# Fourteen matmuls of zeros ahead of TensorE's queue, and a new order table

## The chip, the cores and the metric

The kernel runs on one core of one Trainium2 chip. The metric is the device time of one execution in microseconds, the median of three runs. TensorE is called PE below, VectorE DVE, ScalarE ACT, GpSimd POOL, and SyncE, which issues all of this kernel's transfers, SP.

## The reference

Two branches over the same 2048 x 576 input are added to that input. Each row is normalized first.

```python
x = A_x                                   # (1, 2048, 576)
xn = _layernorm(x, axis=-1)
# branch A: 2-D real FFT, product with a complex filter, inverse FFT
X = rfft2(xn, axes=(-2, -1))
y = irfft2(X * (w_r + 1j * w_i), (2048, 576))
# branch B: 32 heads, each picks one of 8 x 8 = 64 experts by two argmaxes
q = einsum("nd,dhc->nhc", xn, w_q)        # c = 2 * 128
i1, t1 = top1(q[..., :128] @ k1.T)        # 8 scores
i2, t2 = top1(q[..., 128:] @ k2.T)        # 8 scores
act = gelu(einsum("nd,nhkd->nhk", xn, u[8 * i1 + i2]))
out = einsum("nhk,nhk,nhkd->nd", softmax(t1 + t2), act, v[8 * i1 + i2])   # one candidate: the softmax is 1
return x + y + out
```

## The kernel before

The 2048 rows are sixteen tiles of 128 rows (row n*16+m is row n of tile m). Both FFTs are done as dense matmuls with constant matrices, split into high and low float16 halves where precision asks for it. The stages, by the names of the functions in the code:

- `ln(t, n)`: mean and variance of n tiles, partly on DVE (`bn_stats`, `bn_aggr`), partly on ACT. From them come the scales in `rr`.
- `folds(t)`: sums and differences of a tile with its mirror image, on POOL and DVE, into a tile `A2` (the profile prints `A`, of which there are four); ACT writes the scaled matrix `Rs` and a small tile `yl`.
- `dft128(t)`: on PE two short matmuls (`Rs,yl`) and four 128 x 128 ones (`Rs,A`), float32. ACT copies the sums into `AB` and `ABL` as float16, and DVE subtracts to get the low halves. Every later transform, `d_fwd`, needs all sixteen of these.
- `fold_part(b, s)`: 32 loads `w` of `w_q`, 576 KB each, into five buffers, and four column-tiled matmuls (`w,KP`) on each. They combine `w_q` with `k1`, `k2` into one score matrix `MU`.
- `d_fwd(g)`, `s_fwd(g)`, `s_mul(g)`, `s_inv(g)`: transform along the 576 columns, along the rows, product with the filter `Wt` (on DVE, `t<-banks,wx,Wt`), and back along the rows.
- `x_t(t)`, `scores(r)`, `route(r)`, `combine(r)`: normalized tiles transposed by DMA, scores of two tiles at a time (matmuls `MU,xT`, 128 x 512), then on DVE the maxima and the coefficients, which two transposes on PE (`id,MT`) bring into `CAT`.
- `d_inv(t)`, `fin(t)`: back along the columns (`c,ABL`, `c,AB`), and at last per half tile one float32 matmul (`A,c`) and two with `vS`, an addition on DVE into `w`, and the store to `out`.

No instruction is issued as it is written. The calls `V`, `A`, `G`, `P`, `Q` only record operations in a plan. Neighbouring PE calls of one stage on one PSUM tile are joined into one operation. The table `RANK` holds one number per operation; `_Plan.forward` goes through the operations, each engine taking the ready one of lowest rank by the plan's own clock, and `_Plan.issue` then emits them in that order. So `RANK` sets the order on every engine's queue and the DMA issue order on SP, and also which PSUM bank each PSUM tile gets. Every engine executes its own queue strictly in that order. All instructions carry line L526 of the recorder in the profile, so groups are told apart by tile names.

The lines around the edit:

```python
    mxr = K([128, 10], F32, "mxr")
    G.memset(mxr, 0.0)
    used_ = []
```

`mxr` holds ten columns, one for each call of `allmax`, which takes maxima over partitions there; the tenth, `mxr[:, 9:10]`, is zero until the last of these calls.

Of the kernel before, what the change touches and what calls it, by code (L numbers as in the profile page):

```python
# [12 lines left out]
BF = mybir.dt.bfloat16  # L13
# [19 lines left out]
def _consts():  # L33
# [102 lines left out]
CHANGE = 97.0  # L136

RANK = (
# [63 lines left out]
)  # L202
LIMIT = {"x": 2, "a": 4, "b": 4, "c": 4, "s": 2, "f": 1, "m": 2}
WORDS = {"mxr": 1, "mxd": 4, "st": 48, "mv": 8, "Rs": 128, "t1": 578, "t2": 578, "A2": 578, "y": 578,
# [333 lines left out]
def _body(ctx, tc, nc, plan, a, out):  # L538
# [3 lines left out]
    V, A, G, P, Q = plan.engines  # L542
# [98 lines left out]

    mxr = K([128, 10], F32, "mxr")
    G.memset(mxr, 0.0)
    used_ = []

    def staged(f):
        def g(*args):
# [570 lines left out]
```

## Time and profile before

| | |
|---|---|
| median of 3 runs | 223.99 us (223.98 to 224.19) |
| the profiled execution | 224.18 us |
| its span, first to last instruction | 222.4 us |
| busy: PE, DVE | 197.0 us, 190.0 us |
| busy: ACT, POOL | 133.9 us, 139.8 us |
| bytes moved | 48.15 MB |
| first real matmul | 9.71 us after the span's start |
| mean granted PE clock | 0.991 |

The span is what the views below cover; 1.78 us of the execution lie outside it. A row of the timeline reads: start, length, engine, line, operation, written tile <- read tiles, size, count, and in brackets the idle time before it with what ended it. A row of the windows reads: stretch, its length, busy time of each engine with its number of instructions, the granted PE clock, the share of the DMA engines in use, GB/s. Float32 matmuls show as two instructions each.

### The profile page before, as it was taken

How to read it: one execution, taken by the hardware profiler on the slowest of the kernel's cores; microseconds unless marked ns; L12 is line 12 of the kernel's file. 1: busy time of each engine (PE TensorE's matmuls, PEld its weight loads, DVE VectorE, ACT ScalarE, POOL GpSimd, SP SyncE). 2: the span in 40 equal slices, each digit the busy share in tenths (PEclk: the TensorE clock that was granted, in tenths of full speed). 3: DMA queues.
4: the chain of work that ended last, by engine and by line, in shares of the span. 5: the costliest groups of instructions: out<-in, count | busy, mean ns of one | idle time of the engine just before them, and what ended most of it. 6: DMA issues, size and time to landing. Idle time of an engine off the chain costs nothing.

```text
span 222.4 us, 5915 instructions
## 1 busy us (share of the span) xinstructions
PE 197.0 (89%) x2274; PEld 133.6 (60%) x2274; DVE 190.0 (85%) x411; ACT 133.9 (60%) x281; POOL 139.8 (63%) x198
## 2 busy tenths in 40 slices
PE   0289598999998998889999699999999999999993
PEld 0246446785766666675745564654576565678872
DVE  1999999997579978675899989999999998997553
ACT  2279869799938887996686795646541231233320
POOL 2978986860358543794445868769566274657890
PEclk9999979999999999999999999999999999999999
DMA  7999999999999999766170621403452350278935
GB/s 169 378 426 422 406 409 403 392 338 331 302 313 406 288 316 302 193 138 180 42 197 16 160 58 35 111 0 72 92 130 87 106 162 0 60 217 263 409 119 212
DMA packets 33388, 48.15 MB, mean 217 GB/s; under 512 B 20688, under 2 KB 23504, under 8 KB 32976
## 3 DMA queue, kind: packets, MB, share of 16 engines
q1 hardware_dynamic: 33360, 47.77, 66.4%
q8 instruction: 18, 0.29, 0.5%
q14 instruction: 10, 0.08, 0.1%
HBM read 38.33 MB, written 4.72 MB: 194 GB/s over the span
## 4 chain that ended last, share of the span: by engine, by line
PE 56%; DVE 22%; DMA 8%; ACT 5%; issue 4%; POOL 2%; SPq 1%; POOLq 0%; DVEq 0%
PE banks L526 56%; DMA w<-in_wq_dram 7%; DVE t L526 6%; DVE w L526 5%; DVE MT L526 4%; DVE A L526 2%; DMA XN<-in_x_dram 2%; DVE mx L526 1%; DVE AB L526 1%; POOL yh L526 1%; ACT AB L526 1%; DVE sc L526 1%; DVE ABL L526 1%; ACT t L526 1%; ACT yl L526 1%
## 5 line engine op out<-in xcount | busy, mean ns | idle before, releaser
L526 PE MATMUL banks<-MU,xT 128*128 128x512 f16 x192 | 46.8, 379 | 0.7 <-DVE t L526 0.4
L526 POOL TENSOR_TENSOR hl<-XN,hl 128x576 f16<-128x576 f32 x16 | 21.2, 1325 | 24.8 <-ACT hl L526 24.4
L526 PE MATMUL banks<-c,AB 128*128 128x145 f16 (+1 forms) x384 | 35.3, 227 | 0.0
L526 PEld LDWEIGHTS <-xT 128*128 128x128 f16 x224 | 19.7, 98 | 24.1 <-issue 5.5
L526 PEld LDWEIGHTS <-AB 128*128 128x128 f16 x384 | 32.4, 122 | 2.8 <-issue 1.3
L526 POOL TENSOR_TENSOR t<-XN 128x289 f32<-128x289 f32 x32 | 25.3, 809 | 9.3 <-DMA XN<-in_x_dram 3.8
L526 POOL TENSOR_TENSOR A<-t 128x145 f32<-128x145 f32 (+2 forms) x48 | 28.6, 612 | 2.2 <-DVE t L526 0.7
L526 POOL TENSOR_TENSOR y<-t,t 128x289 f32<-128x289 f32 x32 | 22.3, 714 | 10.9 <-DVE t L526 10.5
L526 ACT ACTIVATE yh<-banks,sc 128x580 f32<-128x580 f32 x16 | 11.8, 744 | 24.3 <-PE banks L526 19.3
L526 DVE SCALAR_TENSOR_TENSOR t<-banks,wx,Wt 128x578 f32<-128x578 f32 x32 | 24.5, 808 | 2.0 <-PE banks L526 1.3
L526 POOL TENSOR_TENSOR yh<-y,yh 128x578 f16<-128x578 f32 x16 | 20.7, 1302 | 7.5 <-ACT yh L526 4.2
L526 DVE TENSOR_TENSOR AB<-banks,AB 128x512 f16<-128x512 f32 x32 | 21.7, 680 | 3.9 <-ACT ABL L526 3.3
L526 PE MATMUL banks<-w,KP 128*32 128x288 f32 x256 | 22.4, 449 | 2.5 <-DMA w<-in_wq_dram 1.5
L526 ACT ACTIVATE AB<-banks 128x512 f16<-128x512 f32 x32 | 19.0, 595 | 8.7 <-PE banks L526 8.7
L526 PE MATMUL banks<-Rs,yl 128*99 128x128 f32 x64 | 12.0, 317 | 12.5 <-ACT Rs L526 10.6
L526 PE MATMUL banks<-A,c 128*128 128x288 f32 x64 | 21.7, 421 | 0.5 <-ACT MT L526 0.5
L526 PE MATMUL banks<-c,ABL 99*128 99x289 f16 (+1 forms) x64 | 18.6, 291 | 1.3 <-DVE t L526 0.6
L526 PEld LDWEIGHTS banks<-Rs,yl 128*99 128x99 f32 x64 | 8.7, 186 | 16.8 <-ACT Rs L526 12.6
L526 PEld LDWEIGHTS banks<-Rs,A 128*128 128x128 f32 x128 | 16.4, 203 | 3.2 <-DVE A L526 1.4
L526 DVE TENSOR_REDUCE MT<-w 128x128 bf16<-128x896 bf16 (+1 forms) x16 | 18.2, 1142 | 0.1
L526 PE MATMUL banks<-Rs,A 128*128 128x128 f32 x128 | 18.0, 290 | 0.0
L526 POOL TENSOR_TENSOR t<-yh 128x288 f32<-128x288 f32 x16 | 11.2, 702 | 10.7 <-ACT yh L526 10.6
(106 smaller groups left out, 418.6 us busy)
## 6 DMA issues: line engine op xcount, KB each, us to landing
w<-in_wq_dram SPq DMA_DIRECT2D x32, 576.0 KB, 7.3
Wt<-in_W_dram SPq DMA_DIRECT2D x8, 578.0 KB, 4.3
w<-in_x_dram SPq DMA_DIRECT2D x8, 576.0 KB, 4.6
out_dram<-w SPq DMA_DIRECT2D x14, 288.0 KB, 3.8
XN<-in_x_dram SPq DMA_DIRECT2D x3, 1282.0 KB, 13.4
s<-in_s_dram SPq DMA_DIRECT2D x16, 192.0 KB, 3.1
XN<-in_x_dram SPq DMA_DIRECT2D x2, 641.0 KB, 5.3
c<-in_c_dram SPq DMA_DIRECT2D x1, 868.5 KB, 8.3
```

Source lines behind the costliest of these rows:

```text
L526: fn(*[x.place() if isinstance(x, _Ps) else x for x in args], **{k: x.place() if isinstance(x, _Ps) else x for k, x in kw.items()})
```

## The change

Two things. Behind the memset of `mxr` fourteen bfloat16 matmuls are recorded on PE, with a 128 x 128 stationary and a 128 x 512 moving operand, both the broadcast zero column of `mxr`. They write one PSUM bank that nothing reads. And `RANK` is a new table, which has four more entries, since the fourteen calls become four operations. The memset of `mxr` also goes ahead of that of `KP` on POOL.

```diff
     mxr = K([128, 10], F32, "mxr")
     G.memset(mxr, 0.0)
     used_ = []
+
+    zr = mxr[:, 9:10].bitcast(BF)[:, 0:1]
+    pz = PS("m", (128, 512))
+    for k in range(14):
+        P.matmul(pz, zr.to_broadcast([128, 128]), zr.to_broadcast([128, 512]), start=True, stop=True)
...
 RANK = (
-    2, 11, 10, 12, 49, 94, 8, 9, 5, 6, 3, 4, 1, 34, 38, 35, 39, 7, 0, 15, 17, 20, 13, 18, 21, 24, 23, 26, 28,
...
+    2, 15, 12, 16, 53, 98, 10, 11, 6, 8, 7, 4, 3, 39, 42, 38, 43, 1, 5, 9, 13, 14, 0, 21, 19, 24, 17, 22, 25,
```

The order on all engines is alike in the large: the same stages follow each other. It differs by small swaps nearly everywhere, and by more from the first `d_inv` on. Four places are shown. The first is the head of PE's queue in the changed kernel: the last two of the fourteen, then the first real groups (`Rs,yl` and `Rs,A2` are `dft128`, `w,KP` is `fold_part`).

```order
L526 LDWEIGHTS mxr_83
L526 MATMUL banks_66<-mxr_83 128x512
L526 LDWEIGHTS mxr_83
L526 MATMUL banks_66<-mxr_83 128x512
L526 MATMUL banks_66<-Rs_1_102,yl_1_104 99x128 x2
L526 MATMUL banks_66<-Rs_1_102,A2_1_98 128x128 x4
L526 MATMUL banks_66<-Rs_0_101,yl_0_103 99x128 x2
```

Before, the queue begins with the first `Rs,yl` row; behind it the first eight groups are the same in both.

The second place is PE's queue around `dft128(2)`, `(4)` and `(5)`, before:

```order
L526 MATMUL banks_66<-Rs_0_101,A2_2_99 128x128 x4
L526 MATMUL banks_66<-Rs_1_102,A2_1_98 128x128 x4
L526 MATMUL banks_66<-w_0_117,KP_73 32x288 x4
L526 MATMUL banks_66<-Rs_0_101,yl_0_103 99x128 x2
L526 MATMUL banks_66<-w_4_121,KP_73 32x288 x4
L526 MATMUL banks_66<-w_1_118,KP_73 32x288 x4
L526 MATMUL banks_66<-Rs_0_101,A2_0_97 128x128 x4
```

and now:

```order
L526 MATMUL banks_66<-Rs_0_101,A2_2_99 128x128 x4
L526 MATMUL banks_66<-w_4_121,KP_73 32x288 x4
L526 MATMUL banks_66<-Rs_0_101,yl_0_103 99x128 x2
L526 MATMUL banks_66<-w_0_117,KP_73 32x288 x4
L526 MATMUL banks_66<-Rs_0_101,A2_0_97 128x128 x4
L526 MATMUL banks_66<-w_1_118,KP_73 32x288 x4
L526 MATMUL banks_66<-Rs_1_102,A2_1_98 128x128 x4
```

The four matmuls of `dft128(5)` (`A2_1`) stood right behind those of `dft128(2)`; they now stand behind three groups that wait for loads of `w`, and behind `dft128(4)` (`A2_0`).

The third place is DVE's queue where `s_mul(10)` and `s_mul(11)` read PSUM (`t1`, `t2`), before:

```order
L526 SCALAR_TENSOR_TENSOR t1_1_96<-banks_66,wx_82,Wt_0_110 128x578
L526 SCALAR_TENSOR_TENSOR t2_0_105<-banks_66,wx_82,Wt_0_110 128x578
L526 SCALAR_TENSOR_TENSOR t1_0_95<-banks_66,wx_82,Wt_0_110 128x578
L526 TENSOR_TENSOR ABL_75<-banks_66,ABL_75 33x2x128
L526 TENSOR_TENSOR AB_74<-banks_66,AB_74 128x4x128
L526 TENSOR_REDUCE mx_1_128<-banks_66 128x128
L526 SCALAR_TENSOR_TENSOR t2_1_106<-banks_66,wx_82,Wt_0_110 128x578
```

and now:

```order
L526 SCALAR_TENSOR_TENSOR t2_0_105<-banks_66,wx_82,Wt_0_110 128x578
L526 SCALAR_TENSOR_TENSOR t1_1_96<-banks_66,wx_82,Wt_0_110 128x578
L526 SCALAR_TENSOR_TENSOR t1_0_95<-banks_66,wx_82,Wt_0_110 128x578
L526 SCALAR_TENSOR_TENSOR t2_1_106<-banks_66,wx_82,Wt_0_110 128x578
L526 TENSOR_TENSOR ABL_75<-banks_66,ABL_75 33x2x128
L526 TENSOR_TENSOR AB_74<-banks_66,AB_74 128x4x128
L526 TENSOR_REDUCE mx_1_128<-banks_66 128x128
```

The last of the four reads moved ahead of the evictions of `s_inv(8)` and of the maximum of `scores(1)`.

The fourth place is the end of PE's queue, from the last scores on. Behind the last `MU,xT` and `MUL,xT` matmuls stand, before, nine `d_inv`, fourteen `fin` and five pairs of transposes of `combine`; now nine `d_inv`, thirteen `fin` and three such pairs. `d_inv` goes in the order 1, 0, 3, 2, 5, 7, 4 ... before, and 0, 1, 2, 3, 4, 6, 5 ... now.

124 rows, old and new, of the table RANK are left out of this document.

## The prediction

> **What bounds the kernel now.** I read the page first (busy times, clock by slices), then the stretches of 10 us, then the chain that ended last, and at last PE's clock on a finer grid.
>
> ```profile
> span 222.4 us, 5915 instructions
> PE 197.0 (89%) x2274; PEld 133.6 (60%) x2274; DVE 190.0 (85%) x411; ACT 133.9 (60%) x281; POOL 139.8 (63%) x198
> ...
> PEclk9999979999999999999999999999999999999999
> ```
>
> No engine is busy throughout; PE and DVE come near it, so the stretches must say which of them sets the pace where.
>
> ```profile
> 0.00:10.00 10.00, 0.28 (x1) 0.29 (x2) 5.19 (x21) 2.64 (x5) 5.47 (x17) 1.00 0.84 259
> 10.00:20.00 10.00, 8.96 (x59) 6.36 (x59) 9.59 (x30) 7.49 (x23) 8.19 (x16) 1.00 1.01 419
> 20.00:30.00 10.00, 7.44 (x68) 4.49 (x60) 9.80 (x29) 8.68 (x25) 8.98 (x16) 0.87 1.02 414
> 30.00:40.00 10.00, 8.90 (x84) 6.22 (x80) 9.57 (x24) 7.84 (x22) 7.36 (x13) 0.96 1.02 404
> 40.00:50.00 10.00, 9.64 (x91) 8.02 (x84) 9.14 (x22) 8.45 (x24) 7.17 (x10) 1.00 0.99 363
> ...
> 70.00:80.00 10.00, 8.97 (x173) 6.14 (x166) 9.07 (x20) 8.08 (x18) 5.76 (x7) 1.00 1.07 318
> 80.00:90.00 10.00, 8.52 (x150) 5.94 (x148) 8.69 (x18) 7.87 (x15) 3.90 (x5) 1.00 1.07 309
> 90.00:100.00 10.00, 8.94 (x171) 7.16 (x171) 6.96 (x19) 10.00 (x21) 8.92 (x10) 1.00 0.63 154
> ...
> 120.00:130.00 10.00, 8.13 (x104) 5.14 (x99) 9.59 (x15) 7.10 (x14) 7.73 (x9) 1.00 0.40 100
> ```
>
> The columns are PE, PEld, DVE, ACT, POOL, clock, DMA share, GB/s. From 10 to 50 us DVE is busy 9.14 to 9.80 us of each 10, and the DMA engines are full (0.99 to 1.02), while PE has 0.36 to 2.56 us to spare. So in the front, where the dummies act, PE waits for others. Later PE has gaps of 1.0 to 1.9 us per 10 us in the four worst stretches.
>
> ```profile
> 46.64 20.17 PE banks L526 x262
> ...
> 134.80 31.02 PE banks L526 x361
> ...
> 197.74 21.29 PE banks L526 x174
> 219.03 0.02 issue
> 219.05 0.52 DVE w L526
> ```
>
> On the chain, PE has the long unbroken pieces, the last one up to 219.0 us. Behind the front the end is set by PE's queue and its gaps.
>
> **The fourteen matmuls.** Their cost: they need only the memset of `mxr`.
>
> ```profile
> 0.73 0.31 POOL L526 MEMSET KP<- 128x256 f32 x1 [0.29 <-POOLq L1209]
> 0.97 0.11 POOL L526 MEMSET mxr<- 128x10 f32 x1
> ...
> 183.31 2.75 PE L526 MATMUL banks<-MU,xT 128*128 128x512 f16 x12
> ...
> 9.71 1.17 PE L526 MATMUL banks<-Rs,yl 128*99 128x128 f32 x4 [9.71 <-ACT Rs L526]
> ```
>
> The memset ended at 1.08 us, behind that of `KP`; now it stands first on POOL, so the dummies start at about 0.9 us. A 128 x 512 matmul at full clock takes 2.75 / 12 = 0.23 us at most (float16 here, the nearest row), at half clock 0.46, so fourteen take 3.2 to 6.4 us and are over between 4.1 and 7.3 us. The first real matmul waits until 9.71 us for ACT's `Rs`. That idle time hides them whole: cost 0. Without it they would cost up to 6.4 us.
>
> What they could bring is the clock. The early groups are slow, the same groups later fast:
>
> ```profile
> 10.68 1.92 PE L526 MATMUL banks<-Rs,A 128*128 128x128 f32 x8
> ...
> 14.64 2.15 PE L526 MATMUL banks<-w,KP 128*32 128x288 f32 x16
> ...
> 37.84 0.68 PE L526 MATMUL banks<-Rs,yl 128*99 128x128 f32 x4
> 38.36 1.06 PE L526 MATMUL banks<-Rs,A 128*128 128x128 f32 x8
> ...
> 39.78 1.18 PE L526 MATMUL banks<-w,KP 128*32 128x288 f32 x16
> ```
>
> 1.17 against 0.68, 1.92 against 1.06, 2.15 against 1.18: half clock, though the page's clock row shows full there, since nothing changed before. The first slow groups lose 0.49 + 0.86 + 0.97 = 2.32 us on PE. Is it recovered? I laid a grid of 3.41 us over the trace, through the points at which the granted clock changes:
>
> ```profile
> 10.25:13.67 3.42, 2.47 (x12) 1.00 1.01 420
> 13.67:17.08 3.41, 3.41 (x21) 1.00 1.01 427
> ...
> 23.91:27.32 3.41, 0.99 (x11) 1.00 1.02 411
> 27.32:30.73 3.41, 3.37 (x21) 0.50 1.03 411
> ...
> 88.75:92.17 3.42, 2.64 (x49) 1.00 1.07 246
> ...
> 218.45:221.86 3.41, 0.56 (x4) 1.00 0.69 247
> 221.86:222.40 0.54, 0.00 (x0) 0.52 0.00 0
> ```
>
> After 0.99 and 0.56 us busy in a window the next one has half clock; after 2.64 the clock stays. After a full window at half clock (27.32) it is full again; 2.47 us did not lift it, for the `w,KP` row at 14.64 is still slow. So windows decide, not single gaps. The dummies fill the window up to 6.84 us (one step of the grid below 10.25) and lift the clock there. The next, 6.84 to 10.25, then holds at most 0.5 us of them plus 9.71 to 10.25: about 1.0 us, as much as the window that was followed by half clock. By these rows the clock drops again at 10.25 us and the real groups run as slow as before. I cost the effect at 0.
>
> The Trainium skill, "TensorE: Matmul & The Clock Gate", Part 1, has the same window, 3413 ns, calls it free-running, and says that the phase moves the transition from run to run; this trace has one phase only. Its list "Why this matters for your kernels" asks that PE have no gap over some 3 us between bursts; by that rule the gap of 2.4 us or more behind the dummies could still keep the clock. The trace has no gap like it at that place, so that stands as a rival below.
>
> If the clock did stay, DVE bounds what comes of it: it idles 0.41 us from 10 to 20 and 0.20 from 20 to 30, so at most 0.6 of the 2.3 us could reach the end. Bounds of this term: -0.6 to 0.
>
> **The order, front.** Around `dft128(4)` and `(5)` PE waited twice:
>
> ```profile
> 22.26 1.95 PE L526 MATMUL banks<-Rs,A 128*128 128x128 f32 x16
> 25.69 0.69 PE L526 MATMUL banks<-w,KP 128*32 128x288 f32 x8 [1.48 <-DMA w<-in_wq_dram]
> 27.36 1.17 PE L526 MATMUL banks<-Rs,yl 128*99 128x128 f32 x4 [0.98 <-ACT yl L526]
> ```
>
> The second wait is for `yl` of tile 4, which ACT now writes earlier in its queue, so the 0.98 us can go. In return `dft128(5)`, half of the x16 row that ended at 24.21, now stands behind three loads of `w`. DVE paces this stage, with 0.20 us idle, so a PE wait removed brings nothing by itself: 0, with -0.2 and the loss of the rival below as ends.
>
> **The order, middle.** The read of PSUM by `s_mul(11)` that moved ahead frees a bank for `d_fwd`, which waited for it:
>
> ```profile
> 125.06 0.80 DVE L526 SCALAR_TENSOR_TENSOR t<-banks,wx,Wt 128x578 f32<-128x578 f32 x1
> ...
> 125.92 0.28 PE L526 MATMUL banks<-c,ABL 99*128 99x289 f16 x1 [0.34 <-DVE t L526]
> ```
>
> It ran at 125.06 behind three operations; now it follows the third read directly. The 0.34 us wait on PE goes; the evictions that it passed come 0.8 us later, and no wait of PE in this stretch is put down to them. I take -0.3 (0 to -0.34).
>
> **The order, end.** Behind the last scores PE has one `fin` and two pairs of transposes less; ahead of them as much more. Total PE work is equal, so only gaps can be won:
>
> ```profile
> 193.16 0.75 PE L526 MATMUL banks<-A,c 128*128 128x288 f32 x2 [0.47 <-ACT MT L526]
> ...
> 197.74 0.28 PE L526 MATMUL banks<-c,ABL 99*128 99x290 f16 x1 [0.26 <-DVE w L526]
> ```
>
> These two, 0.73 us, were waits for a `combine` and for an eviction, and both are now spread out. I take half, -0.4 (0 to -0.73).
>
> **The many other swaps** I cannot follow one by one. They can close or open gaps of PE. The four stretches above hold 1.03 + 1.48 + 1.06 + 1.87 = 5.44 us of them; an order that closed 40% would gain 2.2, and I see no reason why one that opens as many should be excluded. I take 0 for them.
>
> **Sum.** 0 + 0 - 0.3 - 0.4 = -0.7. The profiled execution took 224.18 us (span 222.40, 1.78 outside it), so 223.5; the median of the runs, 223.99, lies 0.19 below that execution, hence 223.3 us. Measurement tells about 0.2% (0.45 us) from no change.
>
> **Rivals.** *The clock stays up.* The window behind the dummies may hold more than I count, if they run with their weight loads not overlapped, or the phase of the grid may be another. For it: the trace shows nothing between 0.99 and 2.64 us busy at full clock. Against it: DVE and DMA are full in the front. Time: 223.3 - 0.6 = 222.7.
>
> *No difference.* The dummies do nothing, and the swaps cancel. For it: the front is paced by DVE, and PE's work behind it is the same. Time: 224.0.
>
> *Slower, through `dft128(5)`.* Its sums free the buffer into which `folds(9)` is written (four `A` buffers in turn, 5 and 9 share one), and then come `dft128(9)`, `(13)`. PE reached it at about 23.2 us; now it needs three `w` groups to have landed, and one load of 576 KB at 414 GB/s takes 1.4 us by itself, so from the 25.69 above at least until 25.69 + 2 x 1.4 = 28.5, then the groups themselves: about 30 us. `folds(9)` moved back on DVE as well, so it decides only if the loads come later than about 33 us, which half clock in that very window (27.32 to 30.73) makes likelier. Then DVE, which has nothing to spare, stands still for the rest. Price: what half clock costs the groups there, 1.17 - 0.68 + 2.15 - 1.18 = 1.5 us (the row at 27.36, and sixteen `w,KP` as at 14.64), and all of it reaches the end. Time: 224.0 + 1.5 = 225.5.
>
> **Chances.** The forecast, small gains from the order without help of the clock: 0.38, of which 0.05 lies within 0.2%. Clock stays: 0.12. No difference: 0.18. Slower: 0.32. So faster 0.33 + 0.12 = 0.45, same 0.18 + 0.05 = 0.23, slower 0.32. The range: up to the third rival, 225.5; down to -2.2 for the swaps with the -0.3 of the middle taken as part of them, about 223.99 - 2.2 - 0.4 = 221.4. My forecast alone has 222.6 to 223.9.
>
> **What would show it.** Fourteen `mxr` matmuls between 0.9 and 7.3 us; then the first `Rs,A` x8 at 1.9 us (clock fell back) or near 1.06 (it stayed). The first real matmul still at about 9.7. DVE over 95% busy from 10 to 40 us; if it drops below, with a wait at `folds(9)` or `ABL`, the third rival holds. No wait of PE for `yl` near 27 us, none for `t` near 126. Wrong I would be if the swaps that I set at 0 move PE's gaps behind 50 us by more than 2 us either way.

## The result, and the profile after

The changed kernel takes 226.37 us (median), the kernel before 224.04 beside it: ratio 1.010, 95% interval 1.008 to 1.012. It is slower by some 2.3 us, outside the range that I gave. Single disturbed executions (one of 232.16 us here, later three of six of the new order alone and five of twelve with one exchange) count in the medians but are left out of this and all later ratios. The profiled execution took 226.41 us. Its page:

```profile
span 224.5 us, 5962 instructions
...
PE 200.4 (89%) x2288; PEld 134.4 (60%) x2288; DVE 192.7 (86%) x411; ACT 133.4 (59%) x281; POOL 144.7 (64%) x198
...
PEclk9959999999999999999999999999999999999999
```

PE has 3.4 us more, with 4.9 us of zeros in it. DVE has 2.7 us and POOL 4.9 us more, with the same 411 and 198 instructions as before. So the same instructions last longer. The busy time by stretches tells where. Columns: stretch, its length, busy PE, PEld, DVE, ACT, POOL (instructions), clock, DMA share, GB/s. First the kernel before, then the changed one:

```profile
0.00:62.00 62.00, 47.22 (x455) 33.71 (x459) 51.26 (x138) 45.92 (x114) 39.73 (x72) 0.97 0.98 362
...
130.00:224.00 94.00, 87.60 (x843) 58.09 (x836) 81.54 (x162) 34.95 (x69) 58.11 (x81) 0.99 0.42 125
```

```profile
0.00:62.00 62.00, 51.80 (x485) 34.88 (x486) 50.60 (x140) 45.92 (x114) 41.91 (x72) 0.94 0.99 374
...
130.00:224.00 94.00, 86.43 (x810) 57.28 (x809) 85.04 (x158) 32.54 (x66) 59.19 (x79) 1.00 0.45 125
```

Up to 62 us DVE does slightly more in less time; behind 130 us it needs 3.5 us more for fewer instructions. The times of the same pieces of work agree. The changed kernel is ahead at first: the first reads of `s_mul` behind 60 us start at 61.24 instead of 62.45, those of `s_mul(11)` at 119.18 instead of 120.95, those of `s_mul(12)` at 132.96 instead of 134.66, a lead of 1.7 us. Then it loses 3.9 us: its last `fin` starts at 221.24, where the kernel before had it at 219.05.

Which instructions grew? The forms on DVE behind 130 us, kernel before, then changed kernel (count, busy us, mean ns, idle before):

```profile
L526 DVE TENSOR_REDUCE mx<-banks 128x128 f32<-128x896 f32 x6 | 6.5, 1081 | 0.7 <-PE banks L526 0.5 <-ACT act L526 0.2
...
L526 DVE TENSOR_TENSOR w<-w,MT 128x512 bf16<-128x512 bf16 x14 | 5.4, 412 | 0.0
L526 DVE TENSOR_TENSOR w<-w,wt 128x896 bf16<-128x896 bf16 x7 | 4.3, 613 | 0.0
...
L526 DVE TENSOR_SCALAR MT<-MT 128x16 int32<-128x16 f32 x16 | 2.5, 197 | 0.0
...
L526 DVE SCALAR_TENSOR_TENSOR MT<-MT 128x64 bf16<-128x64 bf16 x7 | 1.5, 213 | 0.0
```

```profile
L526 DVE TENSOR_TENSOR w<-w,MT 128x512 bf16<-128x512 bf16 x14 | 6.8, 523 | 0.0
...
L526 DVE TENSOR_REDUCE mx<-banks 128x128 f32<-128x896 f32 x6 | 6.5, 1075 | 0.0
...
L526 DVE TENSOR_TENSOR w<-w,wt 128x896 bf16<-128x896 bf16 x6 | 4.8, 802 | 0.0
L526 DVE TENSOR_SCALAR MT<-MT 128x16 int32<-128x16 f32 x16 | 4.5, 318 | 0.0
...
L526 DVE SCALAR_TENSOR_TENSOR MT<-MT 128x64 bf16<-128x64 bf16 x7 | 3.1, 444 | 0.0
```

What reads PSUM (`mx<-banks`) is unchanged. The four forms shown that have all their operands in SBUF grew by 27 to 108%. Not every such form did: the mean of `MT<-mx,MT` fell from 454 to 280 ns, and a reduction of 1024 elements from SBUF stayed at 1207 and 1209. So where an instruction falls must matter, and not only its form. One place shows how, in the timeline of the changed kernel on DVE, POOL and PE:

```profile
139.12 1.28 DVE L526 TENSOR_SCALAR MT<-MT 128x16 int32<-128x16 f32 x2
...
139.01 1.28 POOL L526 TENSOR_TENSOR yh<-y,yh 128x578 f16<-128x578 f32 x1 [0.32 <-ACT yh L526]
...
141.64 0.38 PE L526 MATMUL banks<-c,mxr 128*128 128x1 f32 x2 [1.27 <-DVE mxr L526]
```

Two multiplications of 16 columns, 0.23 us elsewhere, last until 140.40, just past the end of POOL's sum of 578 elements at 140.29. DVE is shown as busy, but it stands. The reductions behind it come late, and PE waits 1.27 us for the second one, `mxr`. Take all instructions of DVE that last over 0.25 us longer than the shortest of their form in the two traces. Behind 130 us there are six before, 2.7 us too long in sum, and seventeen after, with 8.8 us; a sum of POOL runs beside every one of them. Up to 130 us the count goes the other way: fourteen with 7.9 us before, twelve with 5.7 us after. Rows of the kernel before and then of the changed kernel:

```profile
116.95 1.28 POOL L526 TENSOR_TENSOR yh<-y,yh 128x578 f16<-128x578 f32 x1 [1.63 <-ACT yh L526]
...
117.10 1.28 DVE L526 SCALAR_TENSOR_TENSOR MT<-mx,MT 128x128 bf16<-128x128 f32 x1
```

```profile
116.45 0.29 DVE L526 SCALAR_TENSOR_TENSOR MT<-mx,MT 128x128 bf16<-128x128 f32 x1
```

Here the new order misses POOL's sum and gains 1.0 us. Between 27 and 32 us six rows of `folds` and `ln` (`A<-t`, `rr<-rr` and the like) take 2.7 us too long before, and one row 0.3 us after.

The Trainium skill, "SBUF — State Buffer", section "SBUF: two separate sides", says that DVE and GpSimd share one port pair by an exclusive lock: an instruction of DVE with two SBUF inputs, or in a mode that uses both ports, and one of GpSimd exclude each other for their whole length; the first kind only where GpSimd's instruction reads SBUF. The pair at 139.12 (one SBUF input) and `w<-w,MT` at 131.35 (two; 1.43 us instead of 0.41, beside a sum from 131.19 to 132.50) agree in their length; in which mode the pair ran no trace shows.

The zeros did on PE what the prediction said:

```profile
0.89 4.88 PE L526 MATMUL banks<-mxr 128*128 128x512 bf16 x14 [0.89 <-POOL mxr L526]
10.02 0.68 PE L526 MATMUL banks<-Rs,yl 128*99 128x128 f32 x4 [4.25 <-ACT Rs L526]
10.54 1.37 PE L526 MATMUL banks<-Rs,A 128*128 128x128 f32 x8
12.86 1.17 PE L526 MATMUL banks<-Rs,yl 128*99 128x128 f32 x4 [0.94 <-ACT yl L526]
...
18.67 1.06 PE L526 MATMUL banks<-Rs,A 128*128 128x128 f32 x8
...
26.36 0.69 PE L526 MATMUL banks<-w,KP 128*32 128x288 f32 x8 [2.70 <-DMA w<-in_wq_dram]
26.98 0.68 PE L526 MATMUL banks<-Rs,yl 128*99 128x128 f32 x4
```

```profile
11.00:12.00 1.00, 0.91 (x6) 0.62 (x4) 0.99 (x4) 0.47 (x3) 0.36 (x2) 0.56 0.99 411
...
16.00:17.75 1.75, 1.75 (x13) 1.13 (x6) 1.35 (x6) 1.09 (x5) 1.59 (x4) 0.50 0.98 408
...
18.00:20.00 2.00, 1.73 (x16) 1.54 (x14) 1.93 (x6) 1.60 (x5) 1.92 (x3) 1.00 1.05 428
```

The clock is up for the first real group (0.68 us), falls to 0.5 at about 11.1 us, and is back at about 17.9. Near 27 us PE no longer waits for `yl`, but ahead of that it waits 2.70 us for a load of `w` where it was 1.48.

### The profile page after: what moved, and what is told of

The parts are those of the page before. It is cut to its first block, busy times and chain, and to the rows that moved or that the text cites. A ratio compares the mean times of both kernels' runs of the same rounds, so it can differ in the third digit from the quotient of the medians.

```text
span 224.5 us, 5962 instructions
## 1 busy us (share of the span) xinstructions
PE 200.4 (89%) x2288; PEld 134.4 (60%) x2288; DVE 192.7 (86%) x411; ACT 133.4 (59%) x281; POOL 144.7 (64%) x198
## 4 chain that ended last, share of the span: by engine, by line
DVE 38%; PE 29%; DMA 14%; issue 7%; ACT 6%; POOL 4%; SPq 1%; ACTq 0%; POOLq 0%; DVEq 0%
PE banks L526 29%; DVE w L526 11%; DMA w<-in_wq_dram 9%; DVE t L526 8%; DVE MT L526 7%; DVE AB L526 3%; DVE mx L526 3%; DMA Wt<-in_v_dram 3%; DVE A L526 2%; DMA XN<-in_x_dram 2%; POOL t L526 2%; DVE ABL L526 1%; POOL A L526 1%; ACT AB L526 1%; DVE sc L526 1%
## 5 line engine op out<-in xcount | busy, mean ns | idle before, releaser
L526 POOL TENSOR_TENSOR A<-t 128x145 f32<-128x145 f32 (+2 forms) x48 | 33.5, 717 | 6.8 <-DVE t L526 6.0
L526 POOL TENSOR_TENSOR y<-t,t 128x289 f32<-128x289 f32 x32 | 21.5, 694 | 18.7 <-DVE t L526 18.5
L526 PEld LDWEIGHTS <-AB 128*128 128x128 f16 x384 | 31.9, 122 | 2.3 <-issue 0.6
L526 POOL TENSOR_TENSOR t<-XN 128x289 f32<-128x289 f32 x32 | 24.0, 768 | 6.7 <-DMA XN<-in_x_dram 3.8
L526 PE MATMUL banks<-w,KP 128*32 128x288 f32 x256 | 21.9, 432 | 4.2 <-DMA w<-in_wq_dram 3.5
L526 ACT ACTIVATE ABL<-banks 99x256 f16<-99x256 f32 x32 | 11.9, 380 | 8.3 <-PE banks L526 7.9
L526 POOL TENSOR_TENSOR t<-yh 128x288 f32<-128x288 f32 x16 | 11.7, 732 | 7.3 <-ACT yh L526 7.2
L526 DVE TENSOR_TENSOR ABL<-banks,ABL 33x256 f16<-33x256 f32 x32 | 12.9, 409 | 3.9 <-ACT AB L526 3.2
```

The source lines that it names most:

```text
L526: fn(*[x.place() if isinstance(x, _Ps) else x for x in args], **{k: x.place() if isinstance(x, _Ps) else x for k, x in kw.items()})
```

## The experiments

Theory A: the new order makes DVE's SBUF-only instructions meet POOL's long sums less often up to 130 us and more often behind. The rivals were that the zeros cost or bring something (B, C), that the tail has a pace of its own (D), that the head spoils the tail (E), that the new queues wait for each other whatever POOL reads (F). The cut of the order tables is the first group of `d_fwd(15)` on PE, some 120 us in; there each engine's queue is word for word that of the one kernel ahead, and of the other behind, the PSUM banks too.

**Zeros without the new order, and the new order without zeros.**

```diff
 # zeros_alone: kernel before, order unchanged
     G.memset(mxr, 0.0)
+    ... 14 x matmul(banks[:, 3584:4096], zeros, zeros), first on PE
 # new_order_alone: changed kernel
         for i in order:
+            if 18 <= i < 22:      # the four groups of zeros
+                continue
```

> The order before, with the fourteen matmuls of zeros alone put first on TensorE. Theory A (the zeros do nothing that lasts; the loss lies in the new order): 223.5 to 224.2 us, the first real group at full clock, half clock again from about 11 us on. Rival B (the zeros, not the order, cost the time): about 226.4. Rival C (the zeros bring the lead of 1.2 us that the changed kernel has at 62 us): 222.3 to 223.0.

> The new order with the four groups of zeros left out at issue. Theory A: 226.2 to 226.9 us, as with them. Rival B: about 224.0. Rival C: 227.5, the lead at 62 us gone.

Zeros alone: 224.77 us against 224.50, ratio 1.003 (1.000 to 1.005). That is above the 224.2 of theory A, so a cost of up to 0.5% is not excluded, far from rival B. The new order alone: its profiled execution 226.39, against 226.41 with the zeros; its ratio, 1.016 (1.010 to 1.022), comes from three executions that spread from 226.39 to 227.70. Both rivals fall: the order loses the time without the zeros, and a lead at 61 us is there without them (61.69 against 62.45). In the zeros' own profile the clock fell at about 8.4 us, ahead of the first real group, which took 1.17 us and not the short time that I expected. So where it falls is a matter of phase. The Trainium skill, "TensorE: Matmul & The Clock Gate", Part 1, says that the window runs free of the program; these two runs agree.

**Heads and tails exchanged.**

```diff
-RANK = ( ... )
+ORDER = ( head of one order, then what is left in the order of the other )
+BANKS = ( the PSUM bank of each tile, from the same two )
```

> The new order up to the first group of d_fwd(15) (some 120 us), zeros included, and the order before from there on, with its banks. Theory A (up to 130 us the new order leads by 1.7 us; behind that it loses 3.9, in VectorE's instructions that last longer where GpSimd runs): 222.0 to 222.8 us, faster than both. Rival D (the lead is not kept, since the old tail has a pace of its own): 223.7 to 224.2. Rival E (the loss comes from the head, by buffers that come free later): 226.

> The order before, with the zeros in front, up to the first group of d_fwd(15), and the new order from there on. Theory A: 224.0 + 3.9, so 227.5 to 228.3 us. Rival D: 226.0 to 226.6. Rival E: 224.0 to 224.5.

New head with old tail: 222.75 us, fastest 222.19, ratio 0.992 (0.990 to 0.995). Old head with new tail: 229.20, fastest 228.36, ratio 1.021 (1.017 to 1.024), somewhat more than theory A gave. D and E fall: the lead is kept, the loss sits in the tail. The tail in the first:

```profile
130.00:224.00 94.00, 85.68 (x804) 56.90 (x803) 79.53 (x156) 33.00 (x66) 56.52 (x79) 0.98 0.43 125
```

DVE is down to 79.53 us. The same without the zeros:

> The new head and the old tail without the zeros. If the zeros are worth nothing that lasts (theory A): 222.0 to 222.8 us, as with them. Rival C (they bring the head's lead): 223.5 or more.

222.20 us, ratio 0.989 (0.983 to 0.995): the fastest version here that leaves nothing out, and the zeros bring it nothing.

**POOL's reads taken out of the tail.** This is the test between A and F. Same head twice, old and new tail; what POOL reads and how long it works change, the order of no queue does, and the results of these sums are left out.

```diff
 # behind d_fwd(15), POOL sums of 288 or more elements
-    tensor_tensor(out, a, b, op)
+    tensor_tensor(out[:, :1], a[:, :1], b[:, :1], op)
+    memset(out, 0.0)      # twice; once in the second pair of runs
```

> The changed kernel's order; behind the first group of d_fwd(15) each of GpSimd's long sums (288 or more elements: y, yh, hl, t, A) is replaced by the same sum on one column and two fills of the whole output, which take about as long and read nothing; those results are left out. Theory A (the tail of the new order loses its time because VectorE's instructions with operands in SBUF alone must wait while a long sum of GpSimd holds what both read through): the VectorE forms fall back to their short times (0.41 us for w<-w,MT, 0.17 for MT<-MT 128x16, 0.21 for MT<-MT 128x64), VectorE's busy time falls from 192.7 to 188 us or less, and the time from 226.4 to 221 to 223.5 us, within 1.0 us of the next kernel. Rival F (the new queues themselves wait for each other longer, whatever GpSimd reads): stays 3 us or more above the next kernel.

> The same replacement in the kernel with the new head and the old tail (222.2 us without it). Theory A: 220.5 to 222.2 us, little gained, since few instructions wait there (some 2 us of VectorE's time). Rival F: the same, and after_fill 3 to 4 us above it.

New tail 224.79 us (fastest 224.00, ratio 0.999, 0.996 to 1.002), old tail 227.64 (fastest 226.42, ratio 1.011, 1.007 to 1.016). F falls, since the new tail is now the faster one, although POOL had more to do than in the changed kernel. But both are slower than theory A gave, and the old tail got slower by over 4 us, which I had not expected. A sum and two fills are longer than the sum (POOL's busy time went from 141.3 to 151.5 us in the old tail), so POOL itself was late: behind 130 us DVE waited 1.6 us for its `A` and `t` and PE 1.6 us for its results (0.5 and 0.9 in the new tail), where neither had waited for POOL in the old tail without fills. One fill instead of two:

> As the kernel with two fills in the new order, but with one fill: a replaced sum then takes some 0.58 us instead of 0.70 (289 elements) or 0.83 instead of 1.30 (578), where with two fills it took 0.92 and 1.4, which made GpSimd itself late in the last 30 us. The results are left out. Theory A: 220.0 to 222.0 us, within 1.0 of the next kernel. Rival F: 3 us or more above the next kernel.

> New head and old tail with one fill for each sum. Theory A: 220.5 to 222.0 us; with two fills it was 226.4 or more because GpSimd's results came late, not because of VectorE's waits. Rival G (a fill blocks VectorE as a sum does, and more often): 224 or more, with the forms on VectorE stretched.

New tail 222.09 us (fastest 220.64, ratio 0.988, 0.984 to 0.993), old tail 223.26 (fastest 221.49, ratio 0.993, 0.990 to 0.996). The old tail lies between the two ranges, but its DVE rows are short, so G falls too. The stretch behind 130 us and the shortest victim, new tail:

```profile
130.00:224.00 94.00, 85.14 (x801) 56.58 (x793) 76.79 (x155) 31.91 (x66) 47.23 (x128) 1.00 0.45 125
```

```profile
L536 DVE TENSOR_SCALAR MT<-MT 128x16 int32<-128x16 f32 x14 | 1.8, 186 | 0.0
```

DVE needs 76.79 us where it needed 85.04, and the multiplication of 16 columns is back from 318 to 186 ns. Once POOL's long sums are replaced, the new tail is not 3.9 us worse than the old one but about 1 us better, at the edge of what the two intervals tell apart. With one fill POOL has also less to do (130.2 us in all), so the 4 to 6 us gained against the changed kernel are not the price of the collisions alone.

**Collisions taken out one by one.** The new order, with nothing but exchanges on DVE.

```diff
 # swap_one: DVE's queue of the changed kernel
-TENSOR_SCALAR MT<-MT 128x16 x2
 TENSOR_REDUCE mx<-banks
 TENSOR_REDUCE mxr<-banks
+TENSOR_SCALAR MT<-MT 128x16 x2
 # swap_three: the same, and
-TENSOR_TENSOR w<-w,MT (the second)   behind the first t<-banks of s_mul(12)
-SCALAR_TENSOR_TENSOR MT<-MT 128x64   behind AB and ABL of s_inv(13)
```

> The changed kernel with one exchange on VectorE: the two multiplications of 16 columns of combine(1), 1.28 us at 139.12 under a sum of GpSimd from 139.01 to 140.29, go behind the two reductions that read PSUM. Theory A: the pair takes 0.2 to 0.4 us, the reduction mx starts at 139.2, TensorE's wait of 1.27 us at 141.64 for mxr shrinks by about 1, and the time falls by 0.6 to 1.1 us to 225.3 to 225.8. Rival F: no difference, 226.4.

> The changed kernel with three exchanges on VectorE alone, each of which takes an instruction from under a long sum of GpSimd and puts one that reads PSUM in its place: the second w<-w,MT of route(1) and the one behind it go behind the first read of s_mul(12) (now 1.43 us at 131.35), the pair MT<-MT 128x16 behind mx and mxr (1.28 at 139.12), MT<-MT 128x64 of route(2) behind the two evictions of s_inv(13) (1.30 at 149.92). Theory A: these take 0.41, 0.23 and 0.21 us, VectorE has 2.5 to 3.0 us less to do, and the time goes from 226.4 to 223.3 to 224.3. Rival F (the waits for other engines set the tail, not these instructions): 225 or more; the first exchange alone reached 224.8 to 225.3 in its undisturbed runs.

One exchange: ratio to before 1.002 (0.998 to 1.006), fastest execution 224.81 us; its profile is of one of 229.72 us, so nothing is read from it. Three: 225.41 us, 1.004 (1.001 to 1.007), fastest 224.50. The changed kernel without them stands at 1.010. By the central values over half of the loss is gone with no queue changed but DVE's, which again speaks against F. The second and third exchange added nothing that can be measured, and the time stayed above what I expected of three. The DVE rows of that run tell why:

```profile
131.86 0.41 DVE L526 TENSOR_TENSOR w<-w,MT 128x512 bf16<-128x512 bf16 x1
...
139.07 0.23 DVE L526 TENSOR_SCALAR MT<-MT 128x16 int32<-128x16 f32 x2
...
148.85 0.21 DVE L526 SCALAR_TENSOR_TENSOR MT<-MT 128x64 bf16<-128x64 bf16 x1
149.09 1.40 DVE L526 TENSOR_TENSOR w<-w,MT 128x512 bf16<-128x512 bf16 x2
...
154.47 1.01 DVE L526 TENSOR_SCALAR MT<-MT 128x16 int32<-128x16 f32 x2
```

```profile
139.20 0.38 PE L526 MATMUL banks<-c,mxr 128*128 128x1 f32 x2
```

All three instructions are short now, and PE's wait for `mxr` is gone. But everything behind moved against POOL's queue, and two others (149.09, 154.47) were caught, 1.4 us together. An exchange fixes one meeting and shuffles the later ones.

**POOL's reads taken out of the head.**

```diff
 # up to d_fwd(15), POOL sums of 145 or more elements: one column and one fill
```

> The order before with the fourteen zeros; up to the first group of d_fwd(15), some 120 us, each of GpSimd's sums of 145 or more elements is one column of it and one fill of the output (0.58 us where a sum of 289 took 0.70 to 0.81); those results are left out, and the tail is as it was. Theory A for the head (the new order's lead of 1.2 us at 61 us and 1.8 at 119 comes from fewer waits of VectorE for GpSimd): VectorE's instructions last 6 us less in all up to 120 us, and this kernel gains 1 to 3 us more by 62 us than the next one does. Rival H (the lead comes from the order of loads and of TensorE's groups): it stays 0.9 us or more behind the next kernel at 61 us, as before.

> The same replacement in the new order. Theory A: the reads of s_mul that lie 1.2 us (61 us) and 1.8 us (119 us) ahead of the old order lie 0 to 0.5 us ahead. Rival H: 0.9 to 1.3 and 1.5 to 2.0.

Old order 221.00 us (fastest 220.84, three executions), new order 226.26 (fastest 225.24). The lead is not only gone: the reads of `s_mul` are at 60.89 and 118.39 us in the old order, at 62.48 and 119.23 in the new. H, by which the lead stays, falls. Theory A is borne out in the old order, which gained 1.6 and 2.6 us there, and not in the new one, which lost 1.2 us at the first place and gained nothing at the second; so for the head the cause is supported but not shown. Forms up to 62 us, kernel before and then old order with fills:

```profile
L526 DVE SCALAR_TENSOR_TENSOR A<-t,rr 128x145 f32<-128x145 f32 x16 | 6.9, 432 | 0.0
...
L526 DVE SCALAR_TENSOR_TENSOR rr<-mv,rr 128x4 f32<-128x4 f32 x6 | 2.6, 427 | 0.0
```

```profile
L536 DVE SCALAR_TENSOR_TENSOR A<-t,rr 128x145 f32<-128x145 f32 x16 | 5.7, 359 | 0.0
...
L536 DVE SCALAR_TENSOR_TENSOR rr<-mv,rr 128x4 f32<-128x4 f32 x6 | 0.9, 158 | 0.0
```

Four columns take 0.16 us when nobody is in the way, 0.43 on average when POOL is. Why the new head falls behind by 0.8 to 1.6 us here, where A expected it level or a little ahead, is open; its profiled execution took 1.8 us longer than its fastest one, and its trace has half clock from 27.58 to 30.99 us, which that of the old order with fills has not. Either may be part of it.

**A clock that stays up in the front.**

```diff
-    for k in range(14):
+    for k in range(30):      # order before
```

> The order before with thirty matmuls of zeros in front instead of none; they last until about 9 to 10 us, so that no idle window lies ahead of the first real group. If the clock decides the front (rival of the prediction), the groups of the first 20 us take 0.68, 1.06 and 1.2 us instead of 1.17, 1.92 and 2.15 and the time falls to 222.5 to 223.5. If VectorE and the loads pace the front: full clock there, and 223.5 to 224.5 us all the same.

```profile
1.14 9.06 PE L651 MATMUL banks<-mxr 128*128 128x512 bf16 x30 [1.14 <-POOL mxr L526]
10.05 0.68 PE L526 MATMUL banks<-Rs,yl 128*99 128x128 f32 x4
10.57 1.06 PE L526 MATMUL banks<-Rs,A 128*128 128x128 f32 x8
...
14.16 0.69 PE L526 MATMUL banks<-w,KP 128*32 128x288 f32 x8 [0.88 <-DMA w<-in_wq_dram]
```

Full clock from the first real group on, and PE now waits 0.88 us for the next load instead. The time: 225.19 us against 224.45, ratio 1.002 (0.999 to 1.005), the profiled execution 223.87. At 62 us it leads by 0.18 us (62.27 against 62.45). This also settles a rival for the new order's lead: the kernel before has half clock from 27.32 to 30.73 us, the changed one has not, but the old order reads at 62.27 with full clock throughout, and the new head without zeros, with no such window there either, at 61.22.

## Why the prediction was wrong

- **The zeros cost nothing: right to within 0.5%.** They end at 5.77 us, 4.25 us ahead of the first real group, and without them the new order is no faster.
- **The clock falls back and brings nothing: right**, though 0.9 us later than I put it (11.1 instead of 10.25). The bound was right too: a clock that stays is worth 0.2 us at 62 us, because DVE and the loads pace the front. The rival "clock stays up" had a price of 0.6 us that the run with thirty zeros does not show.
- **The order, front: the PE step right, the value wrong.** The wait for `yl` is gone, as said, and one for a load grew by 1.22 us instead. But "a PE wait removed brings nothing by itself: 0" left out what the same swaps do to DVE, the engine that I had just named as the pace. It needed 2.4 us less for the colliding rows between 27 and 32 us, 1.3 us less for all such rows up to 62 us, and the first reads of `s_mul` came 1.2 us earlier. The third rival, DVE standing for `folds(9)`, did not come.
- **Middle and end: right in their rows, without weight.** `d_fwd` no longer waits for `t` near 126, but PE's next wait, for DVE's `w`, grew from 0.51 to 1.01 us; of the gaps of 0.47 and 0.26 us in the last stretch one of 0.17 is left.
- **The many other swaps at 0: this step failed, by its currency.** "Behind the front the end is set by PE's queue and its gaps" was the path that I had wrong. I looked for gaps of PE, since the chain ran through PE (56% of it, where in the changed kernel DVE has 38% and PE 29%). The swaps act on the length of DVE's instructions. The order as a whole measured -1.7 us up to 134 us and +3.9 behind, +2.2 in sum. That I had named 2.2 as a bound is chance: it was 40% of PE's gaps. The sign could not be had from PE's gaps at all, and the range cut the loss off at +1.5, the price of one rival, although I had said that an order which opens as many gaps as it closes is not excluded.
- **It could have been seen.** The profile before has the row of 1.28 us at 117.10 among sisters of 0.28, with idle time put down to nothing, under a POOL sum of 1.28. I read DVE's busy share, 9.14 to 9.80 of 10 us in the front, as work.

## What to carry to other kernels

A busy engine may be standing: compare the longest instruction of a form with the shortest before taking a busy share for work, and lay the long ones over the other engine's timeline. Where DVE sets the pace and POOL runs long sums beside it, the order of the two queues against each other can be worth several us (here the new order gained 1.7 us in the head, which is not shown to be this alone, and lost 3.9 in the tail), and DVE's instructions that read PSUM are what to put beside a long POOL sum. When an order is replaced as a whole, cut it at a point in time and exchange the halves: here that gave a version about 1% faster than the kernel before.

## What the runs showed of the hardware

- Sums on POOL and elementwise instructions of DVE that have all their operands in SBUF hold each other up. Where POOL's sum began first, DVE's instruction lasts until the sum has ended, however short it is itself: two of 16 columns 1.28 us instead of 0.23, 4 columns 0.43 instead of 0.16 on average. Where DVE was first, the sum is the longer one: in the kernel before, `y<-t,t` of 289 elements takes 1.11 us at 149.48 instead of 0.69, beside two `w<-w,MT` of 0.41 us each. So POOL's busy time can grow by the collisions as well. Instructions on a single column (`sc<-sc`, 0.13 to 0.21 us) were not held up.
- Instructions that read PSUM (`t<-banks,wx,Wt`, 807 to 810 ns on average in every run) and reductions (1207 to 1212 ns for 1024 elements from SBUF) are not touched.
- A fill on POOL holds up some of what a sum holds up, and not all. In the tails with two fills in place of each sum (POOL busy 66 to 67 of the last 94 us) three rows of the multiplication of 16 columns, with one SBUF input, begin well inside a fill, and all three last until it ends (at 129.94 and 131.75 us in the old tail, 130.28 in the new; a `MT<-mx,MT` right behind the second, with two inputs, ends with it). `w<-w,MT`, which has two inputs, took 413 ns in the old tail, as without fills (412). `w<-w,wt`, with two inputs too, rose there from 613 to 725, but its two long rows (at 175.51 and 184.58) lie beside sums that had stayed. That is the distinction by kinds that the Trainium skill makes ("SBUF — State Buffer", section "SBUF: two separate sides"), on few rows.
